# A spectral filter and a top-1 MoE on one core: the first two adds of a batch's filtered product on VectorE in place of POOL

## The chip, the core and the metric

The kernel runs on one core of a Trainium2 chip. The metric is the device time of one execution in microseconds (us); less is better. The number shown of a kernel is the median of several executions. A profile is one further execution, recorded by the hardware profiler.

## What is computed

The input `x` is [8, 2496, 256] in fp32: 8 batches, a sequence of 2496, 256 channels. Along the sequence it is filtered in the frequency domain; then every row goes through one of 8 experts.

```
X = rfft(x, axis=1); y = irfft(X * (filt_r + 1j*filt_i), n=2496)
x = y.reshape(19968, 256)
logits = normalized(x) @ normalized(expert_emb).T / tau
e = argmax(logits); gate = softmax(logits)[e]
out = gate * (relu(x @ w1[e]) @ w2[e])        # w1: 256x1024, w2: 1024x256
```

## The kernel before

**The filter.** The sequence of 2496 is 39 x 64, so the transform is done in two factors, each a product with a constant matrix on TensorE. A batch passes three stages, each a generator that yields after a part of a step, so that the steps can be woven between other work.

- `conv_s1` (L450): products with `c1`, results to memory (`SD`).
- `conv_s2` (L573), the stage of the change: for each of 10 steps k it loads a piece `a` (L583) and the step's two filter rows `f` (L591), multiplies by `c2` into a PSUM tile `s` (the product s; L443, from batch 3 on three matmuls on split operands at L448), and makes two halves. `yy` is the PSUM tile times the real filter row, on VectorE (L602). `xs` is a copy with the partition halves exchanged, by ScalarE (L630, L631), which VectorE then multiplies by the sign and the imaginary filter row (L604). The add `yy = yy + xs` follows at L638. Two steps later (`SAL` = 2) the sum is multiplied by `m1` (the product sa; L656 in batches 0 to 2, from batch 3 on L448), copied by ScalarE (L659) and stored to `ZD` (L660). From batch 3 on the operands of both products are first split in an upper part on ScalarE (`yp`, `ap`; L416) and a lower part on VectorE (L417); for the sum that is done one step after the add.
- `conv_sb` (L663): loads from `ZD`, the last product, then per chunk of 128 rows the expert's choice (L768 and on), the ranking of rows within their expert (L833, L836) and a scatter of the rows to the experts' places in a table `XS` (L862), an indirect DMA that POOL issues.

The first batch (0) has its own path (`conv_first`), with an add of its own at L544.

**The experts.** A `Slot` (L972) is 256 rows of one expert; each batch but the last feeds 8 slots while the next batch is being filtered. A slot loads its rows transposed (`xT`, L996) and a small tile of row numbers and gates (`meta`, L998), both on SP's queue. It has four quarters: 12 matmuls up (L1027, from `xT` and the weights `W`), relu to fp16 on ScalarE (L1033), the lower half of the result `h` on VectorE (L1034), and some quarters later the matmuls down (L1055). Its results are scaled by ScalarE (L1062) and scattered to the output by POOL (L962). What is left over of all batches is done at the end in further slots (from about 1100 us).

**The order.** `spread()` (L1142) sets so many conv steps between two quarters of a slot that a batch is done when its experts are. Up to the end of the first batch the order of the instructions is as written. After that the framework orders the instructions of each engine from an estimate of the time line that it makes when the kernel is built. So a line that goes to another engine can move the instructions around it, on all engines. Waits are set by the data.

**Buffers.** PSUM: two tiles for the products s, sa and those of the other conv stages, two for the up matmuls, one for the down matmuls. SBUF: six tiles shared by `xs`, `yy` and the split sums (`hl`), four for filter rows (`f`).

The weights are split into fp16 halves while the first batches run; L302 makes a lower half on POOL.

Of the kernel before, what the change touches and what calls it, by code (L numbers as in the profile page):

```python
# [17 lines left out]
ALU = mybir.AluOpType  # L18
# [39 lines left out]
def moe_spectral_kernel(  # L58
# [16 lines left out]
    nc = tc.nc  # L75
# [284 lines left out]
    def widths(g):  # L360

        return NAG * GROUPS[g] // 2, NK2 * GROUPS[g] // 2
# [46 lines left out]
    def split(hi, lo, pieces):  # L409

        got = []
        for h, a in pieces:
            k, w = a.shape
            o = h.start * D
            xh, xl = hi[:k, o:o + w], lo[:k, o:o + w]
            nc.scalar.copy(xh, a)  # L416
            nc.vector.tensor_tensor(out=xl, in0=a, in1=xh.bitcast(F32), op=ALU.subtract)  # L417
            got.append((h, (xh, xl)))
        return got
# [4 lines left out]
    def asides(nm):  # L424

        return [rowp.tile([P, 2, ROW], F16, tag="rows", name=f"{nm}_{i}").rearrange("p j c -> p (j c)")
                .bitcast(F32R)[:, :2 * D] for i in range(2)]

    def parts_of(c, tag):

        k = c.shape[0]
        tmp = cw.tile([P, P], F32R, tag="hl", bufs=XYB, name=f"{tag}t")[:k]
        lo = const.tile([k, P], F32R, tag=f"{tag}l", name=f"{tag}l")
        nc.scalar.copy(tmp, c)
        nc.vector.tensor_tensor(out=lo, in0=c, in1=tmp.bitcast(F32), op=ALU.subtract)
        hi = const.tile([k, P], F32R, tag=tag, name=f"{tag}h")
        nc.scalar.copy(hi, tmp.bitcast(F32))
        return hi, lo

    def product(out_, c, a):  # L440

        if not isinstance(a, tuple):
            nc.tensor.matmul(out_, c[:a.shape[0]], a, start=True, stop=True)  # L443
            return
        (ch, cl), (xh, xl) = c, a
        k = xh.shape[0]
        for n, (w, b) in enumerate(((ch, xh), (cl, xh), (ch, xl))):
            nc.tensor.matmul(out_, w[:k], b, start=(n == 0), stop=(n == 2))  # L448
# [124 lines left out]
    def conv_s2(g):  # L573

        nb = GROUPS[g]
        _, NK = widths(g)
        sd = SD[g].rearrange("(p k j) c -> p k (j c)", k=NK, j=2 // nb)
        zd = ZD[g].rearrange("(p k j) c -> p k (j c)", k=NK, j=2 // nb)

        def load_a(k):  # L580
            at = cin.tile([P, CW], F32, tag="in", name=f"a{g}_{k}")
            with behind("sp" if g == 1 else ""):
                nc.sync.dma_start(at, sd[:, k])  # L583
            return at

        def load_f(k):
            fts = []
            for k2 in range(k * 2 // nb, (k + 1) * 2 // nb):
                ft = cf.tile([P, 2, D], F32, tag="f", name=f"f{g}_{k2}")
                with behind("sp" if g == 1 else ""):  # L590
                    nc.sync.dma_start(ft, filt[k2])  # L591
                fts.append((k2, ft))
            return fts

        def filtered(out_, in_, fts, ri):

            w = nb
            for n, (k2, ft) in enumerate(fts):
                o, i = out_[:, n * w:(n + 1) * w], in_[:, n * w:(n + 1) * w]
                f = ft[:, ri:ri + 1].to_broadcast([P, w, D])  # L600
                if ri == 0:
                    nc.vector.tensor_tensor(out=o, in0=i, in1=f, op=ALU.mult)  # L602
                else:
                    nc.vector.scalar_tensor_tensor(out=o, in0=i, scalar=sgn_sb[:, k2:k2 + 1], in1=f, op0=ALU.mult,  # L604
                                                   op1=ALU.mult)

        fin = {k: load_f(k) for k in range(2)}
        yield W_GAP
        ain = {k: load_a(k) for k in range(INB - 1)}
        yield W_GAP  # L610
        ys = {}
        lag = SAL if g else 1
        if g == G_S2:
            cons["c2"] = parts_of(cons["c2"], "c2")
        if g == G_SA:
            cons["m1"] = parts_of(cons["m1"], "m1")
        both = slice(0, 2)
        for k in range(NK + lag):
            if k + INB - 1 < NK:
                ain[k + INB - 1] = load_a(k + INB - 1)  # L620
            if k < NK:
                pt = ps_c.tile([P, 2, D], F32, tag="c", name=f"s2_{g}_{k}")
                if g >= G_S2:
                    for u in (0, 1) if k == 0 else (k + 1,):
                        if u < NK:
                            (_, ain[u]), = split(*asides(f"ap{g}_{u}"), [(both, ain[u])])
                product(pt.rearrange("p j c -> p (j c)"), cons["c2"], ain.pop(k))

                xs = cw.tile([P, 2, D], F32, tag="hl", bufs=XYB, name=f"xs{g}_{k}")
                nc.scalar.copy(xs[0:NA], pt[NA:P])  # L630
                nc.scalar.copy(xs[NA:P], pt[0:NA])  # L631
                fts = fin.pop(k)
                yy = cw.tile([P, 2, D], F32, tag="hl", bufs=XYB, name=f"yy{g}_{k}")
                filtered(yy, pt, fts, 0)
                filtered(xs, xs, fts, 1)
                ys[k] = [yy]
                if g:
                    nc.gpsimd.tensor_tensor(out=yy, in0=yy, in1=xs, op=ALU.add)  # L638
                else:

                    ys[k].append(xs)
                if k + 2 < NK:
                    fin[k + 2] = load_f(k + 2)
            yield W_S2
            j = k - 1
            if g >= G_SA and 0 <= j < NK:
                (_, a), = split(*asides(f"yp{g}_{j}"), [(both, ys[j][0].rearrange("p j c -> p (j c)"))])
                ys[j] = [a]
            j = k - lag
            if 0 <= j < NK:  # L650
                zp = ps_c.tile([P, CW], F32, tag="c", name=f"sa_{g}_{j}")
                for n, t in enumerate(ys[j]):
                    if isinstance(t, tuple):
                        product(zp, cons["m1"], t)
                    else:
                        nc.tensor.matmul(zp, cons["m1"], t.rearrange("p j c -> p (j c)"), start=(n == 0),  # L656
                                         stop=(n + 1 == len(ys[j])))
                zt = cst.tile([P, CW], F32, tag="st", name=f"z{g}_{j}")
                nc.scalar.copy(zt, zp)  # L659
                nc.sync.dma_start(zd[:, j], zt)  # L660
            yield W_S2
# [307 lines left out]
    def behind(engine):  # L969
        return tc.issue_after(last[engine].ins) if engine in last else ExitStack()  # L970
# [105 lines left out]
    def later(g):  # L1076

        if g + 1 < NG:
            s1 = conv_s1(g + 1)
            yield from both(conv_sb(g), s1, widths(g + 1)[0] / (2 * widths(g)[0] + 8))  # L1080
            yield from s1
            yield -1
            yield from conv_s2(g + 1)
            yield from later(g + 1)
        else:
            yield from conv_sb(g)
            yield -1
# [177 lines left out]
```

## Time and profile before

| | before |
|---|---|
| median of 3 executions | 1385.8 us (1382.47 to 1387.48) |
| profiled execution: its time | 1380.9 us |
| profiled execution: its span | 1379.0 us |
| mean granted clock of TensorE | 0.954 |
| TensorE (PE) busy | 1257.2 us, 91% |
| VectorE (DVE) busy | 875.8 us, 64% |
| ScalarE (ACT) busy | 705.4 us, 51% |
| POOL busy | 560.8 us, 41% |
| moved by DMA | 218.70 MB, 159 GB/s in the mean |

How to read it: the span runs from the first to the last recorded instruction; the profiled execution's own time is 1.9 us longer, and it lies 4.9 us below the median of the three. Engine times are sums of instruction durations; PE is the matmuls, PEld the loading of their weights, which overlaps them. A wait is the idle time of an engine before an instruction, with the engine, tile and line that released it.

### The profile page before, as it was taken

How to read it: one execution, taken by the hardware profiler on the slowest of the kernel's cores; microseconds unless marked ns; L12 is line 12 of the kernel's file. 1: busy time of each engine (PE TensorE's matmuls, PEld its weight loads, DVE VectorE, ACT ScalarE, POOL GpSimd, SP SyncE). 2: the span in 40 equal slices, each digit the busy share in tenths (PEclk: the TensorE clock that was granted, in tenths of full speed). 3: DMA queues.
4: the chain of work that ended last, by engine and by line, in shares of the span. 5: the costliest groups of instructions: out<-in, count | busy, mean ns of one | idle time of the engine just before them, and what ended most of it. 6: DMA issues, size and time to landing. Idle time of an engine off the chain costs nothing.

```text
span 1379.0 us, 32360 instructions
## 1 busy us (share of the span) xinstructions
PE 1257.2 (91%) x11180; PEld 998.9 (72%) x11180; DVE 875.8 (64%) x2871; ACT 705.4 (51%) x1599; POOL 560.8 (41%) x621
## 2 busy tenths in 40 slices
PE   8773498976999999999999999999999999999997
PEld 6541375554768677877788677867787988999997
DVE  4577586774466757674867576666659722366664
ACT  5463265643564656465556645654656233333333
POOL 2325334346426542753465255526532732222221
PEclk9786699988999999999999999999999999999999
DMA  9453785657687766787678768686763422122221
GB/s 325 126 204 95 159 226 174 194 145 197 212 205 158 224 193 171 213 210 191 179 200 223 180 161 229 185 199 174 202 170 96 114 76 55 48 49 51 45 49 40
DMA packets 221611, 218.70 MB, mean 159 GB/s; under 512 B 125197, under 2 KB 166125, under 8 KB 219520
## 3 DMA queue, kind: packets, MB, share of 16 engines
q1 hardware_dynamic: 193998, 151.93, 42.4%
q0 software_dynamic: 26592, 60.28, 14.4%
q10 hardware_dynamic: 850, 4.32, 1.5%
q8 instruction: 94, 1.54, 0.5%
q14 instruction: 77, 0.63, 0.2%
HBM read 116.37 MB, written 79.60 MB: 142 GB/s over the span
## 4 chain that ended last, share of the span: by engine, by line
PE 54%; issue 12%; DMA 5%; POOL 5%; DVE 1%; ACT 1%; SPq 0%; POOLq 0%; ACTq 0%; DVEq 0%
PE ph L1027 19%; PE po L1055 18%; PE y L443 4%; PE s L443 4%; POOL out_dram L962 3%; PE sa L448 3%; PE tp L753 2%; DMA a<-SD 2%; PE s L448 2%; DMA f<-ZD 2%; PE lp L768 1%; PE sa L656 1%; DMA ZD<-z 1%; POOL XS L862 0%; POOL yy L638 0%
## 5 line engine op out<-in xcount | busy, mean ns | idle before, releaser
L1055 PE MATMUL po<-W,h 128*128 128x256 f16 (+1 forms) x3864 | 499.7, 274 | 3.0 <-ACT o L1062 1.6
L1055 PEld LDWEIGHTS <-h 128*128 128x128 f16 x3864 | 370.2, 98 | 91.1 <-issue 50.3
L1027 PE MATMUL ph<-xT,W 128*128 128x256 f16 x3072 | 403.2, 276 | 32.0 <-DMA xT<-XS 14.5
L1027 PEld LDWEIGHTS <-W 128*128 128x128 f16 x3072 | 298.0, 99 | 120.8 <-issue 78.1
L1033 ACT ACTIVATE h<-ph 128x512 f16<-128x512 f32 (+1 forms) x388 | 203.7, 525 | 307.8 <-PE ph L1027 241.7
L1034 DVE SCALAR_TENSOR_TENSOR h<-ph,h 128x512 f16<-128x512 f32 (+1 forms) x388 | 231.3, 597 | 172.6 <-ACT h L1033 170.4
L962 POOL DMA_INDIRECT out_dram<-o,meta x161 | 172.7, 1073 | 316.1 <-ACT o L1062 270.3
L862 POOL DMA_INDIRECT XS<-rows,ixi x176 | 176.1, 1000 | 143.3 <-issue 78.3
L403 POOL DMA_DIRECT2D in<-in_x x84 | 66.0, 787 | 174.8 <-PE s L443 132.4
L638 POOL TENSOR_TENSOR yy<-yy,xs 128x512 f32<-128x512 f32 x70 | 94.3, 1355 | 100.8 <-DVE xs L604 64.9
L1027 PE MATMUL ph<-xT,wp 128*128 128x128 f16 x1584 | 104.7, 219 | 0.0
L1027 PEld LDWEIGHTS <-wp 128*128 128x128 f16 x1584 | 96.7, 98 | 2.4
L443 PE MATMUL s<-in,c_sb 117*128 117x512 f32 (+1 forms) x168 | 88.0, 609 | 4.4 <-ACT z L659 2.2
L734 ACT ACTIVATE rows<-y 128x256 f16<-128x256 f32 x176 | 66.2, 385 | 49.5 <-PE y L443 49.0
L1015 DVE COPY wp<-W 128x1024 f16 x132 | 60.0, 455 | 49.7 <-PE ph L1027 49.0
L709 DVE SCALAR_TENSOR_TENSOR rows<-y,rr,rows 128x256 f16<-128x256 f32 x176 | 76.9, 477 | 22.2 <-ACT rows L706 21.3
L443 PE MATMUL y<-f,csb_sb 120*128 120x512 f32 (+1 forms) x168 | 82.8, 577 | 7.7 <-DMA f<-ZD 7.7
L706 ACT ACTIVATE rows<-y,rr 128x256 f16<-128x256 f32 x176 | 73.9, 474 | 25.0 <-DVE rr L739 24.0
L602 DVE TENSOR_TENSOR yy<-s,f 128x256 f32<-128x256 f32 x140 | 52.9, 417 | 52.4 <-ACT xs L631 36.6
L1062 ACT ACTIVATE o<-po,meta 128x256 f32<-128x256 f32 x161 | 69.5, 476 | 21.6 <-PE po L1055 17.4
L467 ACT COPY s<-s 128x512 f32<-128x512 f32 x77 | 45.2, 587 | 56.7 <-PE s L443 41.9
L753 PEld LDWEIGHTS <-rows 128*128 128x128 f16 x704 | 48.9, 99 | 27.3 <-issue 23.5
(203 smaller groups left out, 1521.3 us busy)
## 6 DMA issues: line engine op xcount, KB each, us to landing
f<-in_filt SPq DMA_DIRECT2D x148, 256.0 KB
a<-SD SPq DMA_DIRECT2D x70, 256.0 KB
ZD<-z SPq DMA_DIRECT2D x70, 256.0 KB
SD<-s SPq DMA_DIRECT2D x70, 240.0 KB
f<-ZD SPq DMA_DIRECT2D x70, 240.0 KB
in<-in_x POOLq DMA_DIRECT2D x70, 234.0 KB
W<-in_w SPq DMA_DIRECT2D x11, 1024.0 KB
W<-in_w ACTq DMA_DIRECT2D x4, 1024.0 KB
```

The costliest lines, as they stand in the source:

```text
L443: nc.tensor.matmul(out_, c[:a.shape[0]], a, start=True, stop=True)
L638: nc.gpsimd.tensor_tensor(out=yy, in0=yy, in1=xs, op=ALU.add)
L706: nc.scalar.activation(rows[:, i, 0:D], y[:, i], AF.Copy, scale=rr[:, u:u + 1])
L709: nc.vector.scalar_tensor_tensor(out=rows[:, i, D:2 * D], in0=y[:, i], scalar=rr[:, u:u + 1], in1=rows[:, i, 0:D], op0=ALU.mult, op1=ALU.s ...
L753: nc.tensor.transpose(tp[:, i, j], rows[:, i, j * P:(j + 1) * P], ident)
L862: i = nc.gpsimd.indirect_dma_start(out=XS, out_offset=bass.IndirectOffsetOnAxis(ap=ix, axis=0), in_=src, in_offset=None)
L962: i = nc.gpsimd.indirect_dma_start(out=out, out_offset=bass.IndirectOffsetOnAxis(ap=idx, axis=0), in_=o, in_offset=None, bounds_check=NT - ...
L1027: last["pe"] = nc.tensor.matmul(ph[:, fi, :size], wp[:, k * 2 + wh, fi * P:(fi + 1) * P], xT[:, xh * 2 + k], start=(c == 0), stop=(c == 5))
L1033: last["relu"] = nc.scalar.activation(h[:, 0, :, :size], ph[:, :, :size], AF.Relu)
L1034: hd = nc.vector.scalar_tensor_tensor(out=h[:, 1, :, :size], in0=ph[:, :, :size], scalar=0.0, in1=h[:, 0, :, :size], op0=ALU.max, op1=ALU. ...
L1055: nc.tensor.matmul(self.po[:, s], self.hs[fp][:, hh, fi, s * P:(s + 1) * P], self.Wp[:, off + wh * 1024:off + wh * 1024 + D], start=(fp == ...
L1062: nc.scalar.activation(o, self.po[:, s], AF.Copy, scale=self.meta[:, s, 1:2])
```

## The change

One line of `conv_s2` (L638). In the batches 1 to 7 (`g` is the batch) the add of step k goes to VectorE for k = 0 and 1 and stays on POOL for k = 2 to 9.

```diff
                 filtered(xs, xs, fts, 1)
                 ys[k] = [yy]
                 if g:
-                    nc.gpsimd.tensor_tensor(out=yy, in0=yy, in1=xs, op=ALU.add)
+                    (nc.vector if k < 2 else nc.gpsimd).tensor_tensor(out=yy, in0=yy, in1=xs, op=ALU.add)
                 else:
```

The instructions are the same otherwise, but their order differs from batch 1's `conv_s2` on. A row of the order has the line, the operation, and the tiles out<-in with their shape; a name as `yy2_0` or `s2_2_0` carries the batch, then the step, then a number of the build.

The first place is POOL at the start of batch 2's filtered product. Before, after the last scatters of batch 1 (L862) and two of the output (L962):

```order
L862 DMA XS_194<-rows1_10_2884,ixi1_8_3286 178304x258 x2
L962 DMA out_0_dram<-o0_7_0_3720,meta0_7_3262 19968x256
L962 DMA out_0_dram<-o0_7_1_3722,meta0_7_3262 19968x256
L638 TENSOR_TENSOR yy2_0_3503<-yy2_0_3503,xs2_0_3500 128x512
L638 TENSOR_TENSOR yy2_1_3539<-yy2_1_3539,xs2_1_3536 128x512
L638 TENSOR_TENSOR yy2_2_3572<-yy2_2_3572,xs2_2_3569 128x512
```

In the changed kernel the adds of steps 0 and 1 are gone from there; step 2's comes right behind the two output scatters. At the same place TensorE's order reads, before (`sa_2_0` is the product sa of batch 2's step 0, `ph1_0_0` the first quarter of batch 1's first slot):

```order
L443 MATMUL s2_2_1_3534<-a2_1_3458,c2_sb_118 128x512
L443 MATMUL s2_2_2_3567<-a2_2_3460,c2_sb_118 128x512
L656 MATMUL sa_2_0_3594<-yy2_0_3503,m1_sb_119 128x512
L443 MATMUL s2_2_3_3617<-a2_3_3496,c2_sb_118 128x512
L1027 LDWEIGHTS W_168
L1027 MATMUL ph1_0_0_3599<-xT1_0_3445,W_168 128x256
```

and in the changed kernel:

```order
L443 MATMUL s2_2_2_3567<-a2_2_3460,c2_sb_118 128x512
L656 MATMUL sa_2_0_3594<-yy2_0_3503,m1_sb_119 128x512
L443 MATMUL s2_2_3_3617<-a2_3_3496,c2_sb_118 128x512
L656 MATMUL sa_2_1_3632<-yy2_1_3539,m1_sb_119 128x512
L443 MATMUL s2_2_4_3651<-a2_4_3532,c2_sb_118 128x512
L656 MATMUL sa_2_2_3666<-yy2_2_3572,m1_sb_119 128x512
L443 MATMUL s2_2_5_3693<-a2_5_3565,c2_sb_118 128x512
L656 MATMUL sa_2_3_3724<-yy2_3_3622,m1_sb_119 128x512
L1027 LDWEIGHTS W_168
L1027 MATMUL ph1_0_0_3599<-xT1_0_3445,W_168 128x256
```

Five products of the filter have moved ahead of the slot's first matmul.

The second place is SP's queue at the start of batch 3's filtered product, where the filter rows `f3_4` and `f3_5` of step 2 are loaded. Before:

```order
L583 DMA a3_6_5495<-SD3_181 128x512
L998 DMA meta2_0_5540<-XS_194 128x2x2
L591 DMA f3_4_5374<-in_filt 128x512
L591 DMA f3_5_5376<-in_filt 128x512
L996 DMA_TRANSPOSE xT2_0_5538<-XS_194 128x4x256
```

and in the changed kernel:

```order
L583 DMA a3_6_5495<-SD3_181 128x512
L998 DMA meta2_0_5540<-XS_194 128x2x2
L998 DMA meta2_1_5855<-XS_194 128x2x2
L998 DMA meta2_2_6047<-XS_194 128x2x2
L998 DMA meta2_3_6309<-XS_194 128x2x2
L998 DMA meta2_4_6663<-XS_194 128x2x2
L998 DMA meta2_5_6985<-XS_194 128x2x2
L591 DMA f3_4_5374<-in_filt 128x512
```

The small loads of five further slots have moved ahead of the filter rows.

The third place is VectorE in batch 7, in the second slot from the end of batch 5's experts (`h5_6_0` to `h5_6_2` are the lower halves of its first three quarters). Before:

```order
L1034 SCALAR_TENSOR_TENSOR h5_5_3_13505<-ph5_5_3_13492,h5_5_3_13505 128x512
L417 TENSOR_TENSOR yp7_0_1_13675<-yy7_0_13607,yp7_0_0_13674 128x512
L1034 SCALAR_TENSOR_TENSOR h5_6_0_13549<-ph5_6_0_13536,h5_6_0_13549 128x512
L417 TENSOR_TENSOR ap7_3_1_13701<-a7_3_13590,ap7_3_0_13700 128x512
L417 TENSOR_TENSOR yp7_1_1_13737<-yy7_1_13664,yp7_1_0_13736 128x512
L417 TENSOR_TENSOR ap7_4_1_13763<-a7_4_13651,ap7_4_0_13762 128x512
L1034 SCALAR_TENSOR_TENSOR h5_6_1_13587<-ph5_6_1_13570,h5_6_1_13587 128x512
L1034 SCALAR_TENSOR_TENSOR h5_6_2_13646<-ph5_6_2_13633,h5_6_2_13646 128x512
```

and in the changed kernel:

```order
L638 TENSOR_TENSOR yy7_0_13607<-yy7_0_13607,xs7_0_13604 128x512
L1034 SCALAR_TENSOR_TENSOR h5_5_3_13505<-ph5_5_3_13492,h5_5_3_13505 128x512
L638 TENSOR_TENSOR yy7_1_13664<-yy7_1_13664,xs7_1_13661 128x512
L417 TENSOR_TENSOR yp7_0_1_13675<-yy7_0_13607,yp7_0_0_13674 128x512
...
L417 TENSOR_TENSOR ap7_4_1_13763<-a7_4_13651,ap7_4_0_13762 128x512
L602 TENSOR_TENSOR yy7_2_13710<-s2_7_2_13699,f7_4_13613 128x256
L602 TENSOR_TENSOR yy7_2_13710<-s2_7_2_13699,f7_5_13615 128x256
L604 SCALAR_TENSOR_TENSOR xs7_2_13707<-xs7_2_13707,sgn_sb_121,f7_4_13613 128x256
L604 SCALAR_TENSOR_TENSOR xs7_2_13707<-xs7_2_13707,sgn_sb_121,f7_5_13615 128x256
L1034 SCALAR_TENSOR_TENSOR h5_6_1_13587<-ph5_6_1_13570,h5_6_1_13587 128x512
```

Beside the two adds, step 2's products with the filter rows (L602, L604) now stand ahead of the lower half of the slot's second quarter; before, they stood behind that of the third. In batches 5 and 6 step 2's products have moved to the same place, before the second quarter's lower half; in batches 3 and 4 they stood ahead of the next lower half before, too, and have moved only past a split. In batch 1, on TensorE, 13 expert matmuls (12 down, one up) that stood ahead of the ranking of the first chunk (L833) now stand behind it.

## Rows read from the trace of the kernel before

**Rows 1.** The page: its first line, and busy time of each engine.
```profile
span 1379.0 us, 32360 instructions
PE 1257.2 (91%) x11180; PEld 998.9 (72%) x11180; DVE 875.8 (64%) x2871; ACT 705.4 (51%) x1599; POOL 560.8 (41%) x621
```

**Rows 2.** Waits for the add, of TensorE and ScalarE: sum us, count, longest.
```profile
PE sa L656 <- POOL yy L638: 8.9, 1, 8.9
...
ACT yp L416 <- POOL yy L638: 68.5, 44, 5.8
```

**Rows 3.** POOL's add (page, costliest groups); VectorE's lower part of the sum (min/median/max ns).
```profile
L638 POOL TENSOR_TENSOR yy<-yy,xs 128x512 f32<-128x512 f32 x70 | 94.3, 1355 | 100.8 <-DVE xs L604 64.9
...
L417 DVE TENSOR_TENSOR yp<-yy,yp x50: 676/693/1836, 461.3 to 1023.2; 128x512 fp32r<-128x512 f32 x50
```

**Rows 4.** Timeline, batch 2: start, us, engine, operation, count, [idle before <-releaser].
```profile
324.84 0.58 ACT L631 COPY xs<-s 64x512 f32<-64x512 f32 x1
331.65 0.89 POOL L862 DMA_INDIRECT XS<-rows,ixi  x1 [0.30 <-issue]
332.57 0.42 DVE L602 TENSOR_TENSOR yy<-s,f 128x256 f32<-128x256 f32 x1 [0.17 <-DMA f<-in_filt]
335.17 3.73 POOL L638 TENSOR_TENSOR yy<-yy,xs 128x512 f32<-128x512 f32 x3
336.23 1.26 SPq L996 DMA_TRANSPOSE xT<-XS  x1
336.52 2.07 PE L656 MATMUL sa<-yy,m_sb 128*128 128x512 f32 x2 [8.90 <-POOL yy L638]
340.08 2.02 PE L1027 MATMUL ph<-xT,W 128*128 128x256 f16 x17
341.94 1.02 PE L656 MATMUL sa<-yy,m_sb 128*128 128x512 f32 x2
```

**Rows 5.** Windows view, after that wait: seventh figure the granted clock.
```profile
336.50:340.10 3.60, 3.58 (x5) 1.34 (x6) 0.00 (x0) 0.59 (x1) 2.40 (x2) 0.50 0.65 146
```

**Rows 6.** Timeline, batch 3, step 2 and around.
```profile
457.98 0.38 SPq L998 DMA_DIRECT2D meta<-XS  x1
458.41 1.90 SPq L591 DMA_DIRECT2D f<-in_filt  x2
461.30 0.50 PE L448 MATMUL sa<-yp,m1h 128*128 128x512 f32 x1 [2.36 <-ACT yp L416]
463.00 0.76 DVE L602 TENSOR_TENSOR yy<-s,f 128x256 f32<-128x256 f32 x2
465.04 0.77 PE L448 MATMUL s<-ap,c2h 128*128 128x512 f32 x1
```

**Rows 7.** Timeline, batch 4, the same place.
```profile
587.60 2.50 POOL L638 TENSOR_TENSOR yy<-yy,xs 128x512 f32<-128x512 f32 x2
588.35 0.98 DVE L602 TENSOR_TENSOR yy<-s,f 128x256 f32<-128x256 f32 x2 [4.11 <-DMA f<-in_filt]
589.57 0.80 PE L448 MATMUL sa<-yp,m1h 128*128 128x512 f32 x1 [3.08 <-ACT yp L416]
592.95 0.48 PE L448 MATMUL s<-ap,c2h 128*128 128x512 f32 x1
```

**Rows 8.** Timeline, batches 6 and 7, the same place.
```profile
848.50 1.47 PE L1027 MATMUL ph<-xT,W 128*128 128x256 f16 x12 [1.67 <-DVE h L1034]
...
977.64 0.62 ACT L416 CAST yp<-yy 128x512 fp32r<-128x512 f32 x1 [5.79 <-POOL yy L638]
...
980.04 1.47 PE L1027 MATMUL ph<-xT,W 128*128 128x256 f16 x12 [2.27 <-DVE h L1034]
```

**Rows 9.** Timeline, the end of batch 1's filter: a weight half and who waits.
```profile
298.07 2.16 POOL L302 TENSOR_TENSOR W<-W 128x1024 f16<-128x1024 f32 x1
...
300.28 4.45 PE L1027 MATMUL ph<-xT,W 128*128 128x256 f16 x20 [5.20 <-POOL W L302]
```

## The prediction, made before the change was run

> **What bounds the kernel now.** The page comes first: TensorE is busy 91% of a span of 1379.0 us, VectorE 64%, POOL 41% [rows 1]. So what an edit on POOL or VectorE is worth is read from the idle time of TensorE, and the list of TensorE's waits comes next. POOL's add (L638) ends one long wait there, 8.9 us; one engine on, ScalarE waited for the same line 44 times, 68.5 us in all [rows 2]. The third view is the timeline at the places of those waits. In batches 2 to 7 the pattern is one: the first steps of the filtered product come while POOL issues the row scatters of the batch before (L862), so the first adds stand behind them. In batch 2 the last scatter begins at 331.65, and the adds follow at 335.17, three in a row without a pause, while TensorE stands 8.90 us [rows 4]. In batches 3 and 4 TensorE stands 2.36 and 3.08 us for ScalarE's first half of the sum, which waited for the add [rows 6, 7]. In batch 7 the same wait goes round a corner: ScalarE stood 5.79 us at its split of the sum with an expert's activation queued behind, and TensorE got its lower half 2.27 us late; batch 6 has 1.67 us of the same [rows 8]. In batch 1 no matmul waited for the add, and batch 5 shows none either.
>
> **The change part by part.** It takes 14 adds off POOL, two in each of seven batches, of 1355 ns in the mean, and gives VectorE 14. VectorE's price is read from L417, which has the same shape and also two inputs in SBUF: 676 to 1836 ns, median 693 [rows 3]. That is 14 x 0.69 = 9.7 us of work on an engine that idles 36% of the span. I cost it at nothing where nothing that TensorE needs is next in VectorE's queue; if that cover is gone, each add costs its 0.69 us. POOL's saved 19 us are worth nothing by themselves, since the adds of step 2 onward stay behind the scatters. As VectorE runs an add when its own two products are done, the waits above go; the question at each place is what is late next.
>
> The Trainium skill ("SBUF — State Buffer", Who interferes with whom) says that a VectorE instruction with two SBUF inputs contends with a GpSimd instruction that reads SBUF, and that one of them then blocks. The 1836 ns of rows 3 agree with that; it becomes a rival below.
>
> Batch 2. The new order puts four steps (products s of steps 3 to 5, sa of steps 0 to 3) ahead of the first expert matmul, which began at 340.08 with sa of step 0 and s of step 3 done. Five products more of 1.02 us would have made that 340.08 + 5.1 = 345.2. In the changed kernel s of step 3 needs the PSUM buffer of step 2, so the product at 332.57 (whose filter row had just landed) plus one add in front: 332.57 + 0.69 + 0.42 = 333.7. A step then takes a product (1.02 at full clock; 2.07 for the first one after the wait, at a granted clock of 0.50 [rows 5]), two copies of 0.58 and two multiplications of 0.42: 3.0 to 4.1 us. Two steps and two products later the experts begin at 333.7 + 6.0 + 2.0 = 341.7 or 333.7 + 8.2 + 4.1 = 346.0. Against 345.2 that gains 3.5 or loses 0.8; I take 1.0, near the middle. With one filter row late, as in batch 4 (4.11 us [rows 7]), the lower end is -4.9. The transposed expert input, issued at 336.23, lies before all of it. So of 8.90 us some 8 come back as a wait for the chain of steps.
>
> Batch 3. TensorE no longer waits at 461.30, but s of step 3, at 465.04, needs step 2's products at 463.00, and their filter rows. On SP's queue these were issued at 458.41 behind one small load that had waited for the scatters until 457.98 [rows 6]. The new order puts five more such loads ahead: 5 x 0.38 = 1.9 us. So the gain of 2.36 is bounded by a loss of 1.9; I take 0.
>
> Batch 4. SP's order is unchanged up to the filter rows, so step 2's products stay at 588.35 and end at 588.35 + 0.98 = 589.3; s of step 3 can start then instead of at 592.95, its predecessors now running from 586.5 on without the stop. The upper end is 3.6; the new order has ScalarE do more before the copies of the expert output that free the PSUM bank for 13 matmuls, so I take 3.0; nothing is the lower end.
>
> Batches 5 to 7. Batch 7's 2.27 us and batch 6's 1.67 go, as ScalarE's activation is no longer behind a waiting split. But the new order puts step 2's products ahead of the lower half of the slot's second quarter (before, behind it), and these wait for filter rows. I take 2.2 (0 to 2.27) for batch 7, whose rows are loaded early, 1.2 (-1 to 1.67) for batch 6 and -0.5 (-1 to 0) for batch 5, which had no wait to lose.
>
> Batch 1. No wait on the add goes. But 13 expert matmuls that stood before the ranking (L833) of its first chunk now stand behind it: 13 x 0.12 (17 took 2.02 us [rows 4]) = 1.5 us earlier for the first scatters, and behind them for the weight half at 298.07, for which TensorE stands 5.20 us [rows 9]. I take 1.5, with 0 as the lower end.
>
> Sum: 1.5 + 1.0 + 0 + 3.0 - 0.5 + 1.2 + 2.2 = 8.4 us. The profiled execution took 1380.9 us, so its like would take 1372.5; it lies 4.9 us below the median of the three runs, and I put the gain on the median: 1385.8 - 8.4 = **1377.4**. Its own range, with the terms half way to their ends, is 1372 to 1382. The last third of the span, where TensorE has no conv steps, is untouched.
>
> **The rivals.** (1) The filter rows take the places of the waits. For it: SP's order in batch 3, and VectorE's 4.11 us for them in batch 4 [rows 7]; against it: batches 4 and 7 load them early. Terms: 0.5, -1, -1.9, 2.5, -1, -0.5 and 1.5 for batches 1 to 7, in all 0.1 us, 1385.7.
>
> (2) Every wait goes with nothing in its place: the upper ends, 1.5 + 3.5 + 2.4 + 3.6 + 0 + 1.7 + 2.3 = 15.0, so 1370.8. For it speaks that the new order was made with the adds early; against it batch 2's chain.
>
> (3) Slower: VectorE's queue stands at step 2's products, with the expert's lower half behind, which TensorE then lacks. Where: batches 3, 5, 6 and 7, where the order puts it so or the rows are loaded late. Price: 4.11 us each, as long as VectorE stood for such a row in batch 4; 4 x 4.11 - 8.4 = 8.0 slower, 1393.8. It decides against the change from more than two batches on (8.4 / 4.11). Against it: in batch 4 the same wait stands before a lower half already, and TensorE's list shows the add as its cause, not VectorE.
>
> (4) Slower by the port: each moved add meets POOL and takes 1.84 in place of 0.69, on TensorE's path: 14 x 1.15 = 16.1, less 8.4, 1393.5. Against it: the adds now run while POOL issues scatters, and POOL's own adds come later. By the rule of "SBUF — State Buffer" in the Trainium skill contention needs a POOL instruction that reads SBUF; the long durations in rows 3 bear that out only as far as POOL's adds go.
>
> That the change doesn't do what it says is out: the order shows 14 adds on VectorE.
>
> **How the numbers follow.** Forecast 0.52, rival (1) 0.23, (2) 0.12, (3) 0.09, (4) 0.04. About 0.5% (6.9 us) is what a measurement of this kernel can tell from no change, so faster means below 1378.9 and slower above 1392.7. Two thirds of the forecast's own range lie below 1378.9: 0.34, with rival (2) 0.46. Slower takes somewhat more than half of (3) and (4) and a tail of (1): 0.10. The rest, 0.44, is the same. The range goes from 1367 (rival (2) less the 3.3 us by which the fastest run lies below the median) to 1390 (rival (1) with some of (3)); what lies outside is about 2 in 10, most of (3) and (4).
>
> **What would show it.** Right: 14 executions of L638 on VectorE at about 0.7 us, 56 on POOL; TensorE's waits without the 8.90 for POOL, in batch 2 thin conv work for some 8 us instead, first expert matmul of that stretch two or more us later than before; s of step 3 in batch 4 about 3 us sooner after the last scatter; no 2.27 in batch 7; in batch 3 TensorE waits at s of step 3. Wrong: new waits of TensorE for VectorE's lower half (L1034) above 3 us in batches 3, 5, 6, 7; VectorE's adds at 1 us or more; or a stretch before 300 us that is longer than before, where the order changed and no term stands but batch 1's.

## The result, and the profile after

The changed kernel takes 1372.9 us (median of 4 executions, 1365.1 to 1378.5) against 1385.7 us before (4 executions, 1382.5 to 1387.5): 12.9 us less, ratio 0.989 with a 95% interval of 0.985 to 0.993. The forecast was 1377.4 us, in a range of 1367 to 1390. On another chip, with more executions, the ratio was 0.990 (0.986 to 0.993). The profiled execution of the changed kernel took 1374.6 us, 6.3 less than that of before; the one of before, 1380.9 us, lies below all four others, so the pair shows only half of the gain.

The page of the changed kernel, to lay beside [rows 1]:

```profile
span 1372.7 us, 32374 instructions
...
PE 1261.0 (92%) x11180; PEld 998.6 (73%) x11180; DVE 886.5 (65%) x2885; ACT 705.1 (51%) x1599; POOL 546.7 (40%) x607
```

VectorE has 14 instructions and 10.7 us more, POOL 14 fewer. The moved line in the changed kernel (count, then shortest/median/longest in ns):

```profile
L638 POOL TENSOR_TENSOR yy<-yy,xs x56: 1252/1284/1897, 192.2 to 1014.4; 128x512 f32<-128x512 f32 x56
...
L638 DVE TENSOR_TENSOR yy<-yy,xs x14: 674/681/2614, 178.2 to 970.5; 128x512 f32<-128x512 f32 x14
```

The waits of the changed kernel that answer to [rows 2, 6, 8] (sum, count, longest):

```profile
PE ph L1027 <- DVE h L1034: 4.7, 6, 1.0
...
PE sa L656 <- DVE yy L602: 2.9, 2, 2.0
PE s L448 <- DVE yy L602: 2.6, 2, 1.4
...
PE sa L448 <- ACT yp L416: 0.2, 1, 0.2
...
ACT yp L416 <- POOL yy L638: 61.1, 38, 3.7
```

TensorE's 8.9 us for POOL are gone, and its two long waits for ScalarE's split, 5.4 us in all before, are down to 0.2. ScalarE still waits for POOL 38 times, but its longest wait fell from 5.8 to 3.7 us. New are TensorE's waits for VectorE's multiplications (L602); in batch 2 it also waits for the copies behind them.

Batch 2 in the timeline of the changed kernel, against [rows 4]:

```profile
330.80 0.69 DVE L638 TENSOR_TENSOR yy<-yy,xs 128x512 f32<-128x512 f32 x1
...
332.31 1.10 PE L656 MATMUL sa<-yy,m_sb 128*128 128x512 f32 x2 [0.97 <-DVE yy L602]
...
333.44 0.58 ACT L659 COPY z<-sa 128x512 f32<-128x512 f32 x1 [0.90 <-PE sa L656]
334.08 1.12 PE L443 MATMUL s<-a,c_sb 128*128 128x512 f32 x2 [0.68 <-ACT z L659]
...
335.25 0.42 DVE L602 TENSOR_TENSOR yy<-s,f 128x256 f32<-128x256 f32 x1 [2.31 <-PE s L443]
...
335.38 0.88 POOL L862 DMA_INDIRECT XS<-rows,ixi  x1 [0.30 <-issue]
...
337.15 1.85 PE L656 MATMUL sa<-yy,m_sb 128*128 128x512 f32 x2 [1.95 <-DVE yy L602]
...
344.78 2.78 PE L1027 MATMUL ph<-xT,W 128*128 128x256 f16 x24
```

VectorE adds at 330.80, with four scatters still to come on POOL, the last at 335.38, and sa of step 0 runs at 332.31; before, it came 4.9 us after the last scatter's start, now 3.1 us ahead of it. Then the chain of steps begins: 0.68 us for a copy, 1.95 us for the next sum. That sum is late on VectorE itself: its products were done at 332.95, but in the new order its add stands behind step 2's first multiplication, at 335.25, and began at 335.99. The experts start at 344.78.

Batch 3, against [rows 6], has the six small loads, the filter rows behind them, VectorE's wait for these, and TensorE's wait at s of step 3:

```profile
455.71 2.97 SPq L998 DMA_DIRECT2D meta<-XS  x6
...
458.78 0.89 SPq L591 DMA_DIRECT2D f<-in_filt  x2
...
462.56 0.42 DVE L602 TENSOR_TENSOR yy<-s,f 128x256 f32<-128x256 f32 x1 [3.33 <-DMA f<-in_filt]
...
463.76 0.47 PE L448 MATMUL s<-ap,c2h 128*128 128x512 f32 x1 [1.15 <-DVE yy L602]
```

Batch 4, against [rows 7]:

```profile
586.25 0.74 DVE L602 TENSOR_TENSOR yy<-s,f 128x256 f32<-128x256 f32 x2
...
587.48 1.06 POOL L862 DMA_INDIRECT XS<-rows,ixi  x1 [0.30 <-DVE xs L604]
...
588.22 0.48 PE L448 MATMUL s<-ap,c2h 128*128 128x512 f32 x1
...
592.49 0.62 ACT L416 CAST yp<-yy 128x512 fp32r<-128x512 f32 x1 [3.65 <-POOL yy L638]
593.13 0.58 ACT L630 COPY xs<-s 64x512 f32<-64x512 f32 x1
...
595.24 0.47 PE L448 MATMUL s<-ap,c2h 128*128 128x512 f32 x1 [1.42 <-DVE yy L602]
```

Product s of step 3 is at 588.22, before the last scatter is over. Step 2's multiplications ran at 586.25, ahead of the last scatter and without a wait; before, VectorE stood 4.11 us for their filter row, and they ran at 588.35, behind it. But step 2's add is still POOL's and still behind the scatters: ScalarE stands 3.65 us for it with the copies of step 3 queued behind, and TensorE waits 1.42 us at s of step 4.

### The profile page after: what moved, and what is told of

It is laid out like the page before. It is cut to its first block, busy times and chain, and to the rows that moved or that the text cites. A ratio compares the mean times of both kernels' runs of the same rounds, so it can differ in the third digit from the quotient of the medians.

```text
span 1372.7 us, 32374 instructions
## 1 busy us (share of the span) xinstructions
PE 1261.0 (92%) x11180; PEld 998.6 (73%) x11180; DVE 886.5 (65%) x2885; ACT 705.1 (51%) x1599; POOL 546.7 (40%) x607
## 4 chain that ended last, share of the span: by engine, by line
PE 52%; issue 11%; DMA 6%; POOL 4%; ACT 2%; DVE 1%; SPq 0%; POOLq 0%; ACTq 0%; DVEq 0%
PE po L1055 18%; PE ph L1027 18%; PE y L443 4%; PE s L443 4%; POOL out_dram L962 3%; PE tp L753 2%; PE sa L448 2%; PE s L448 2%; DMA f<-ZD 2%; DMA f<-in_filt 1%; PE lp L768 1%; DMA a<-SD 1%; POOL yy L638 1%; DMA out_dram<-o,meta 1%; DMA XS<-rows,ixi 1%
## 5 line engine op out<-in xcount | busy, mean ns | idle before, releaser
L1055 PE MATMUL po<-W,h 128*128 128x256 f16 (+1 forms) x3864 | 496.8, 274 | 5.0 <-ACT o L1062 3.4
L1055 PEld LDWEIGHTS <-h 128*128 128x128 f16 x3864 | 368.9, 98 | 92.7 <-issue 51.0
L962 POOL DMA_INDIRECT out_dram<-o,meta x161 | 173.4, 1077 | 304.2 <-ACT o L1062 264.3
L862 POOL DMA_INDIRECT XS<-rows,ixi x176 | 178.2, 1013 | 140.5 <-issue 90.7
L638 POOL TENSOR_TENSOR yy<-yy,xs 128x512 f32<-128x512 f32 x56 | 76.6, 1369 | 103.4 <-DVE xs L604 56.7
L602 DVE TENSOR_TENSOR yy<-s,f 128x256 f32<-128x256 f32 x140 | 53.6, 418 | 47.1 <-ACT xs L631 33.6
```

The lines of the kernel that those rows point to most:

```text
L638: (nc.vector if k < 2 else nc.gpsimd).tensor_tensor(out=yy, in0=yy, in1=xs, op=ALU.add)
L862: i = nc.gpsimd.indirect_dma_start(out=XS, out_offset=bass.IndirectOffsetOnAxis(ap=ix, axis=0), in_=src, in_offset=None)
L962: i = nc.gpsimd.indirect_dma_start(out=out, out_offset=bass.IndirectOffsetOnAxis(ap=idx, axis=0), in_=o, in_offset=None, bounds_check=NT - ...
L1055: nc.tensor.matmul(self.po[:, s], self.hs[fp][:, hh, fi, s * P:(s + 1) * P], self.Wp[:, off + wh * 1024:off + wh * 1024 + D], start=(fp == ...
```

## The experiments

Theory A: the gain is that the first sums no longer stand behind the scatters. B: VectorE's add is faster, 0.68 for 1.28 us, and every moved add counts. C: the new order was lucky; any new order moves the time by some us. A fourth, rival D, is that VectorE becomes what TensorE waits for. The twelve runs were made on three chips. On two of them the kernel before takes 1494.6 and 1482.4 us; there TensorE also stands where the trace shows no releaser (24.2 us before L1055 alone, in the profile of the kernel before), which it doesn't in the profiles from the others. So only ratios to the kernel before on the same chip are compared. Where a diff shows one added line alone, it is the part of L638 that chooses the engine.

**Without batch 1** (first of the two slower chips).

```diff
-(nc.vector if k < 2 else nc.gpsimd)
+(nc.vector if g >= 2 and k < 2 else nc.gpsimd)
```

> The change without batch 1: the adds of steps 0 and 1 go to VectorE in batches 2 to 7 only, and the order of batch 1 is that of before. In the two traces batch 1 lost 3.5 us (its last product copied 5.4 us later, of which 1.9 were there before the change's reach). Theory A (the gain is the adds no longer standing behind the scatters, and batch 1's new order costs): 3 us under the change, about 1370. If batch 1's loss is only a difference between executions: 1373, as the change. Theory C (any new order moves the time by some us, and this one was lucky): anywhere between 1368 and 1386.

1482.9 us, ratio 0.993 (0.990 to 0.995). The change itself was not run on this chip; elsewhere its ratio is 0.990. That batch 1's part costs something isn't shown, and leaving it out is no better. C isn't told apart by it.

**The sum kept waiting for POOL** (both slower chips). VectorE adds 504 of 512 columns, POOL the other 8 (`flat`, whose definition is left out, views a tile's 2 x 256 columns as 512).

```diff
-nc.gpsimd.tensor_tensor(out=yy, in0=yy, in1=xs, op=ALU.add)
+for q, c in ((nc.vector, slice(8, None)), (nc.gpsimd, slice(8))) if k < 2 else ((nc.gpsimd, slice(None)),):
+    q.tensor_tensor(out=flat(yy)[:, c], in0=flat(yy)[:, c], in1=flat(xs)[:, c], op=ALU.add)
```

> The adds of steps 0 and 1 run on VectorE for 504 of 512 columns, and POOL adds the other 8, so that a sum is whole only when POOL has come to it, behind its scatters. Theory A (the wait on POOL's queue is what was removed): the gain is gone, 1381 to 1388, and TensorE's wait of 8 to 9 us for POOL's add in batch 2 is back. Theory B (VectorE's add is faster than POOL's, 0.69 in place of 1.36 us): the gain stays, 1373 to 1376. Theory C: the order stands nearer the change's than before's, 1373 to 1380.

First 0.995 (0.992 to 0.998), 1485.0 us: between the theories, as half of the gain or more is still there (all seventy adds, below, gave 0.990 on this chip). So it was run again beside the change:

> The moved adds, but 8 of 512 columns left to POOL, once more. Theory A: above the change by 6 to 12 us on the same chip, since the wait for POOL is back (TensorE stood 7.4 us at sa of batch 2 in the first profile of it). Theory C: within 4 us of the change, whose order it mostly has.

1479.1 us, ratio 0.998 (0.995 to 1.001), while the change has 0.990 (0.986 to 0.993) on the same chip, some 10 us less. Batch 2 in the timeline of this second run:

```profile
327.15 0.68 DVE L638 TENSOR_TENSOR yy<-yy,xs 128x504 f32<-128x504 f32 x1
...
332.21 0.89 POOL L862 DMA_INDIRECT XS<-rows,ixi  x1 [0.30 <-issue]
...
335.90 1.62 POOL L638 TENSOR_TENSOR yy<-yy,xs 128x8 f32<-128x8 f32 x3
...
336.20 2.08 PE L656 MATMUL sa<-yy,m_sb 128*128 128x512 f32 x2 [7.77 <-issue]
```

VectorE's part is done at 327.8, the 8 columns come 8 us later behind the scatters, and TensorE's wait is back, 7.77 us (its releaser is not named, but it ends 0.30 us after POOL's first piece begins). The faster add stayed, and the gain went in most part on this chip, in lesser part on the first: for A, against B.

What it tests is batch 2. Measured from the last scatter of batch 1 to its own last scatter, that batch took 135.6 us in the kernel before, 132.7 here and 123.6 in the change, in single profiles on this chip. In batches 3 to 7 the kernel before shows on this chip no wait of TensorE for the split of a sum, and at most 1.2 us for a lower half. So that the gain in those batches hangs on the same wait is not tested by this run; for it there are the runs on the faster chip, below.

**The last two adds instead of the first two** (both slower chips).

```diff
+(nc.vector if k >= 8 else nc.gpsimd)
```

> As many adds go to VectorE as in the change, but those of steps 8 and 9, when no scatter is in POOL's queue. Theory A: no wait of TensorE goes, within 4 us of before, 1382 to 1390. Theory B (each add's shorter time counts): the same gain as the change, 1373. Theory C (order alone): 3 to 13 us off before in either direction.

1486.6 us, ratio 0.996 (0.993 to 0.999): less than the change, but not nothing, as A had it.

> The adds of steps 8 and 9 on VectorE, once more: its 8.0 us under before (ratio 0.9928 to 0.9986) spoke against theory A, which wants 0.997 to 1.003. If that was the chip's scatter, the ratio comes to 0.997 or more here; if order alone can give such gains (theory C), it is again 0.993 to 0.998 or, on another chip, as far off to either side.

1473.2 us, 0.993 (0.989 to 0.996). TensorE's wait in batch 2 is there as before (9.0 us in its profile), so this gain has another cause. A guess, theory L, was that the last step's sum is sooner in memory for the loads of the next stage; the last of the runs below speaks against it as a second gain beside the change's, on another chip. It stays open, as does whether the gain exists on the faster chips, where this kernel was not run alone.

**All seventy adds** (first of the two slower chips).

```diff
+nc.vector.tensor_tensor(
```

> All 70 adds of batches 1 to 7 go to VectorE. Theory A: what is behind the scatters is what the change has already taken, so 1368 to 1377, as the change within 4 us; VectorE has 56 x 0.69 = 39 us more work, under 70% busy. Theory B: five times the change's gain, under 1350. Rival D (VectorE becomes what TensorE waits for): slower than the change by over 4 us, with waits for the lower half (L1034) and for the split (L417) above before's 11 us.

1479.0 us, 0.990 (0.987 to 0.994). Five times as many adds, the same gain: B falls. VectorE is 61% busy, and TensorE's waits for the lower half are 4.9 us (4.0 in the kernel before on the other slower chip): D falls too.

**The change and the kernel before, on the second of the slower chips.**

> The change itself, beside the others on the same chip. The four experiments before ran on a chip on which the kernel before takes 1494.6 us in place of 1385.7, so the change has to be measured there as well. All theories: 0.8 to 1.2% under before on whichever chip it is; on the chip of the four experiments 1479 to 1483 (all adds moved gave 1479.0, without batch 1 1482.9).

1469.3 us, ratio 0.990 (0.986 to 0.993).

> The kernel before, unchanged, as a measure of what two runs of one and the same program differ by: ratio 0.998 to 1.002, and a profile of it on this chip to lay beside the others'. A ratio as far off as 0.996 would mean that the gains of under 0.5% measured here cannot be told from none.

1483.9 us, ratio 1.000 (0.997 to 1.003), over single executions from 1472 to 1495: a ratio of 0.995 can be told from none, one of 0.998 can't.

**Batch 2 alone, all but batch 2, the middle adds, and both ends** (a chip on which the kernel before takes 1388.4 us).

```diff
+(nc.vector if g == 2 and k < 2 else nc.gpsimd)
+(nc.vector if g != 2 and k < 2 else nc.gpsimd)
+(nc.vector if k in (4, 5) else nc.gpsimd)
+(nc.vector if k < 2 or k >= 8 else nc.gpsimd)
```

> Only batch 2's two adds go to VectorE. In the traces TensorE's wait of 8.9 us there goes, and batch 2's filter from its last scatter on is 9 to 10 us shorter. Theory A (that wait is most of the gain): 5 to 10 us under before, ratio 0.993 to 0.9966. Forecast as recorded (8 of the 8.9 us come back as a chain of steps): 1 us under before, ratio 0.998 to 1.001. Theory C (order alone): as mid, whatever that gives.

1385.4 us, 0.998 (0.995 to 1.001). The longest wait of all is gone, and the gain is 3 us, with an interval from 7 less to 1.5 more: nearer the recorded forecast than A's 5 to 10, whose lower part it doesn't exclude.

> The change in all batches but batch 2. Theory A: 3 to 8 us under before (batches 4, 6 and 7 gained, 1 and 3 lost in the traces), ratio 0.9945 to 0.998, and with the gain of only_b2 it adds up to the change's 13. Forecast as recorded: 7.4 us under before, 0.995. Theory C: no sum is to be expected; either may be as good as the change.

1376.3 us, 0.991 (0.988 to 0.994): 12.1 us less, more than either theory gave. The gain is in the other batches, where the longest waits of TensorE on the add, straight or round a corner, were 1.7 to 3.1 us.

> As many adds go to VectorE, those of steps 4 and 5, which are neither behind the scatters nor at the end of the filter. Theory A, and theory L (late gained because the last step's sum is sooner in memory for the next stage's loads): nothing, ratio 0.997 to 1.003. Theory C or B: 0.992 to 0.997, as late.

1392.5 us, 1.002 (0.999 to 1.005). The same number of adds, and nothing: B falls again. C falls as a general rule, with a limit: apart from the moved adds its compute engines run the same lines in the same order as before up to 477 us, in batch 3, and the order differs from there on.

> The first two and the last two adds of batches 1 to 7 on VectorE. If the change's gain (ratio 0.990) and late's (0.9941 in the mean of its two runs) have different causes (A and L), they add: 0.982 to 0.987. If late's gain is order alone (C), no sum: 0.986 to 0.996. Rival D (VectorE becomes a wait): above 0.992.

1374.1 us, 0.989 (0.985 to 0.994). That lies above the sum that A and L together ask for, though the interval reaches into it: what the last two adds gave on the slower chips isn't seen to add to the change. No version beat the change beyond the intervals.

**Where it is gained.** Six profiles were taken where the kernel before takes 1385.7 or 1388.4 us. Each batch is measured from the last scatter (L862) of the batch before, through the last copy of sa (L659), to its own last scatter (batch 7: to the first relu of the 57th slot); the means are over the three kernels in which that batch's first two adds are POOL's, and the three that move them.

| batch | on POOL, us | moved, us | difference | forecast |
|---|---|---|---|---|
| 1 | 187.9 | 188.8 | +0.9 | -1.5 |
| 2 | 123.3 | 117.5 | -5.8 | -1.0 |
| 3 | 132.3 | 135.5 | +3.2 | 0 |
| 4 | 126.2 | 120.5 | -5.7 | -3.0 |
| 5 | 129.8 | 131.4 | +1.6 | +0.5 |
| 6 | 135.1 | 131.0 | -4.1 | -1.2 |
| 7 | 140.5 | 135.9 | -4.6 | -2.2 |

The three values of a mean lie within 4.6 us of each other, so a difference of 1 or 2 us says nothing. The sum is -14.5 us, near the 12.9 that was timed.

How can 12.1 us come from batches whose waits on the add were so short? The windows views answer (length, TensorE's busy time, PEld, VectorE, ScalarE, POOL, granted clock, DMA share, GB/s): first the stretch from 400 to 1110 us, with batches 3 to 7, then, inside it, the stretches at half the clock, all that there are. Middle adds:

```profile
400.00:1110.00 710.00, 687.33 (x5881) 538.91 (x5880) 484.75 (x1746) 403.50 (x951) 322.71 (x371) 0.99 0.69 182
464.40:467.60 3.20, 3.20 (x15) 2.22 (x15) 3.17 (x8) 2.48 (x5) 1.11 (x1) 0.50 1.11 233
519.00:522.20 3.20, 3.20 (x7) 1.49 (x8) 0.34 (x2) 0.84 (x4) 0.00 (x0) 0.50 0.96 291
594.10:597.30 3.20, 3.20 (x15) 1.89 (x15) 3.20 (x5) 2.82 (x7) 2.86 (x4) 0.50 0.17 61
846.70:849.90 3.20, 3.18 (x16) 2.19 (x16) 2.51 (x8) 2.61 (x5) 2.59 (x3) 0.50 0.67 205
990.00:993.20 3.20, 3.17 (x14) 2.39 (x14) 2.38 (x4) 1.93 (x5) 1.46 (x2) 0.50 0.49 92
```

Batch 2 alone:

```profile
400.00:1110.00 710.00, 689.60 (x5893) 541.55 (x5891) 480.76 (x1720) 403.68 (x942) 338.76 (x381) 0.99 0.70 180
515.50:518.80 3.30, 3.30 (x12) 1.62 (x10) 1.40 (x6) 2.61 (x12) 0.00 (x0) 0.50 0.73 206
590.60:593.90 3.30, 3.30 (x13) 1.98 (x14) 3.28 (x7) 3.24 (x7) 0.43 (x2) 0.50 0.27 18
908.00:914.60 6.60, 6.11 (x22) 3.67 (x23) 2.44 (x7) 2.09 (x8) 0.00 (x0) 0.50 0.74 131
986.50:993.20 6.70, 5.74 (x21) 3.98 (x21) 4.64 (x11) 4.63 (x10) 2.19 (x2) 0.50 0.49 119
```

Before:

```profile
400.00:1110.00 710.00, 690.36 (x5969) 546.09 (x5969) 482.94 (x1735) 405.78 (x952) 345.56 (x390) 1.00 0.69 183
463.00:466.30 3.30, 3.30 (x15) 2.20 (x12) 3.30 (x7) 2.10 (x4) 1.59 (x1) 0.50 1.04 253
589.30:592.60 3.30, 3.03 (x12) 1.96 (x13) 3.30 (x5) 2.99 (x7) 3.11 (x3) 0.50 0.15 55
```

The change has none:

```profile
400.00:1110.00 710.00, 696.12 (x6039) 550.44 (x6037) 485.76 (x1737) 406.75 (x952) 339.37 (x381) 1.00 0.69 183
```

All but batch 2 has one, and both ends one of twice the length:

```profile
400.00:1110.00 710.00, 695.14 (x6018) 548.79 (x6018) 492.30 (x1751) 407.84 (x955) 340.73 (x383) 1.00 0.69 184
464.00:467.30 3.30, 3.28 (x12) 2.06 (x12) 3.30 (x6) 0.88 (x2) 1.57 (x1) 0.50 1.02 291
```

```profile
400.00:1110.00 710.00, 696.52 (x6025) 551.38 (x6024) 487.90 (x1746) 407.16 (x946) 324.32 (x370) 1.00 0.69 183
586.10:592.70 6.60, 5.88 (x21) 3.87 (x22) 4.67 (x11) 3.38 (x6) 3.65 (x3) 0.50 0.71 188
```

TensorE's idle time (710 less its busy time) is 22.7, 20.4 and 19.6 us where these batches' first adds are POOL's, and 13.9, 14.9 and 13.5 where they are moved: 6.8 us less in the mean. At half the clock it spends 16, 20 and 7 us against 0, 3 and 7, some 11 us less; half of that time is lost work, 5.5 us. Together that is 12.3 us, against the 12.1 that were timed for all batches but 2 (batch 1 shows no gain in the table).

Not all of this is shown to come from the adds. Three of the stretches at half the clock, at 519 us with the middle adds and at 515 and 908 with batch 2 alone, follow waits of another kind, for the loads from `ZD` of the next stage. In this order (sum, count, longest):

```profile
PE y L443 <- DMA f<-ZD: 2.2, 1, 2.2
PE y L443 <- DMA f<-ZD: 1.8, 1, 1.8
PE y L443 <- DMA f<-ZD: 3.0, 2, 1.8
```

They are 13.1 us of half clock, 2.2 us of the 5.5, and the waits for such loads make up 1.9 us of the 6.8. Without both some 8 us remain. Whether the moved adds also shorten the waits for `ZD` is not shown, so the agreement of 12.3 with 12.1 is in part luck.

On the two slower chips the gain lies elsewhere, by the single profiles from them. There batch 2 takes 132.2 to 135.6 us in the five profiles in which its first sums wait for POOL, and 123.2 to 125.9 in the three in which they don't, 9.6 us less in the mean. Batches 3 to 7 together take 734.7 to 743.1 us and 740.9 to 750.3: no gain.

Batch 7 with its first adds on POOL shows both prices at one place, here in the timeline of the kernel with the middle adds moved:

```profile
984.27 1.47 PE L1027 MATMUL ph<-xT,W 128*128 128x256 f16 x12
...
990.03 2.72 PE L1027 MATMUL ph<-xT,W 128*128 128x256 f16 x12 [2.98 <-DVE h L1034]
```

Twelve matmuls of one shape take 1.47 us before the wait of 2.98 us and 2.72 us after it. With these twelve alone the wait cost 4.2 us, not 3.0.

## Why the prediction was right, and where its steps were off

**The bound and the mechanism** were right: the first sums stood behind the scatters, the kernel with 8 columns left to POOL loses most of the gain on one chip and part of it on the other, and the one with the middle adds moved has none. The time lies in the range, on the forecast side; the forecast gain of 8.4 us is two thirds of the 12.9 measured, and the step that failed is a missing term. That the time came as near has luck in it: by the table batch 2 was underrated by 4.8 us and batch 3 overrated by 3.2.

**The price of a wait** was taken as TensorE's idle time, in batches 3, 4, 6 and 7 without the clock. Only in batch 2 did the working use a product at the granted clock of 0.50 [rows 5]. The half-clock stretches behind the waits of [rows 6, 7], at 463 and 589 us of the kernel before, were in the same view and went unread; each is worth some 1.7 us. Idle time alone gives 6.8 us for batches 3 to 7, against the forecast's 5.9 (3.0 - 0.5 + 1.2 + 2.2); the clock's 5.5 us, of which 3.3 don't follow waits for `ZD`, were not in it.

**VectorE's price**, 0.69 us, was right: median 0.68, and 13 of the 14 adds at most 0.69. Rival (4), the port, was seen once, in batch 1 (below). That the work hides was right too, but for step 1's add in batch 2: all seventy adds cost nothing that shows.

**Batch 2**: right in kind, one of its numbers wrong. The forecast put s of step 3 behind step 2's multiplication and one add, since it would need that step's PSUM buffer. It ran at 334.08, ahead of that multiplication at 335.25, with the buffer that ScalarE had just copied sa from. The experts then began 9.4 us after the start of the last scatter (8.4 before), where 8.4 + 5.1 = 13.5 would have been no gain: 4.1 us, not 1.0, and beyond the recorded upper end of 3.5. Later in that batch TensorE waits 2.1 us for the next stage's loads from ZD (between 350 and 385 us), where the kernel before waits for nothing: the filter is early, what follows it isn't. The stretch as a whole is 5.8 us shorter, yet batch 2 alone gained 3.0 us in the timed runs, with an interval that holds both 1.0 and nothing. How much of the 5.8 is given back later isn't settled. On the slower chips, where batch 2 was not timed by itself, the profiles' 9.6 us make the net of 1.0 look far too small.

**Batch 3** went the way that was forecast: the six small loads delay the filter rows, and TensorE's wait moves to s of step 3, 1.15 us. In size it was worse: the stretch became 3.2 us longer, where the forecast took 0 and had 1.9 as its lower end. Rival (1), the filter rows in the place of the add, happened here, and more strongly in the kernel with all but batch 2: there VectorE stands 4.68 us for the rows in batch 3, TensorE waits 2.8 us for the multiplication behind them, and the half clock at 464 us above follows. In batch 4 of both ends TensorE waits 3.1 us for the same multiplication, with the half clock at 586 us; there VectorE stood 4.11 us at a split (L417) ahead of it, not at filter rows.

**Batch 4**: s of step 3 came at the last scatter's start plus 0.7 us, before plus 6.3 (592.95 against a last scatter at 586.7). That is 5.5 us sooner, where the forecast had some 3: it let step 2's multiplications stay at 588.35, with their wait of 4.11 us for the filter row, and that wait went too. The forecast's reason to take off 0.6 us was a real one, but the wrong queue entry: ScalarE stood 3.65 us for POOL's add of step 2. The stretch as a whole became 5.7 us shorter; the wait of 3.08 us and the clock behind it would make 4.8 of that.

**Batches 6 and 7**: right in kind, too small, since only the longest wait of each was counted, and that without its clock. In batch 7 before, TensorE's waits for the lower half are three, 4.0 us in all between 960 and 1030 us; the changed kernel has none between 955 and 1025. In batch 6 they are 2.5 before and 1.0 after. The fear for the new order there, the multiplications of step 2 ahead of the lower half, showed no new long wait: the longest for a lower half is now 1.0 us. So rival (3) did not occur; rival (2)'s total of 15.0 us was nearer than the forecast's, though not by its reason: not every wait went without a successor.

**Batch 1**: wrong in sign, by a little. The wait for the weight half fell only from 5.20 to 4.6 us, and the stretch is 0.9 us longer, which single executions can't tell from nothing. In the first pair of traces alone the last copy of sa was 5.5 us later, at 248.5 for 243.0, the sign of being wrong that the prediction named for the time before 300 us; measured from the last scatter of batch 0, over three kernels each, that stretch is 0.1 us longer.

## What to carry to other kernels

A short elementwise step on an engine that also issues long runs of indirect DMAs waits behind all of them; move the one or two instances that meet the run, and leave the rest. The longest wait in the list need not hold the most gain: on the faster chip taking 8.9 us away gave 3 us, as the steps behind it were a chain, while the other batches, with waits of 1 to 3 us beside full work, gave 12. Nor is the place of a gain the same on every chip: on the slower ones, by their profiles, it was that of the longest wait. Price a wait of TensorE by its idle time and by the granted clock of the stretch behind it, and check both in windows.

## What the runs showed of the hardware

Single waits of 2.4 to 3.1 us in the stage where TensorE is else over 96% busy were followed by 3.3 us or twice that at half the clock, the lower of its two levels (1.2 for 2.4 GHz): 0.50 at 463 us after the wait of 2.36 us [rows 6], at 589 after that of 3.08 [rows 7], and at 990 after 2.98 in the run above. Shorter ones were too, of 2.2 and 1.8 us, at 519 and 515. Not every wait is: the changed kernel waits 2.7 us once for a load from ZD in that stage and shows no lower clock.

One moved add took 2.61 us in place of 0.68. In batch 1 it began 0.22 us after a POOL instruction that makes a weight half:

```profile
181.81 2.29 POOL L302 TENSOR_TENSOR W<-W 128x1024 f16<-128x1024 f32 x1 [22.42 <-ACT W L301]
182.03 2.61 DVE L638 TENSOR_TENSOR yy<-yy,xs 128x512 f32<-128x512 f32 x1
```

It ends 0.54 us after POOL's, so it seems to have waited for it. It is so in every profile of a kernel that moves this add, seven in all: 2.61 to 2.62 us, begun 0.22 us behind that POOL instruction. The 13 others in the changed kernel took 0.67 to 0.69 us, nine of them while POOL was issuing an indirect DMA. The Trainium skill ("SBUF — State Buffer", Who interferes with whom) says that a VectorE instruction with two SBUF inputs contends with a GpSimd instruction that reads SBUF, and that the order of issue decides which of two blocks. The trace agrees.

One and the same program took 1388 us on one chip and 1482 and 1495 us on two others, with stalls of TensorE there whose releaser no view names and more of its time at half the clock: in the profiles of the kernel before its mean granted clock is 0.926 on the second of the slower chips, against 0.954. Why was not tried.
